# A linear-attention block mixed with a gated MLP: gate and up of both token pairs first, h kept in DRAM, and all down projections as seven block products over three feature groups

## The chip, the cores and the metric

One core of a Trainium2 chip. The time is that of the device in microseconds (us), of the slowest core; the median of 3 runs is 1539.86 us (1535.67 to 1541.33). All data is float32; operands of TensorE are split into a high and a low part of type float32r, and a product of two such operands is the sum of high x high, high x low and low x high.

## The reference

x has 2048 tokens of 576 features. The output mixes a linear attention of 32 heads and a gated MLP with 4608 hidden features by one sigmoid gate per token:

```python
g = sigmoid((x * gate_w).sum(-1, keepdims=True))
# a: linear attention
q, k, v = split_heads(x @ wqkv)
pq, pk = phi(q), phi(k)            # phi(t) = where(t > 0, t + 1, exp(t)) + 1e-6
kv, z = sum_s pk v, sum_s pk
a = merge_heads((pq @ kv) / (pq @ z + 1e-6)) @ wo
# b: gated MLP
h = gelu(x @ w_gate) * (x @ w_up)
b = h @ w_down
return g * a + (1 - g) * b
```

## The kernel before

The instructions stand on each engine in the order in which the program writes them; nothing is reordered. Five engines work at once (TensorE, VectorE, ScalarE, GpSimd, and SP, which issues most transfers), each strictly in its own order, and wait for one another by semaphores.

**Keys, values, queries (to about 180 us).** Projections, Gram matrices and the head states are made; the token blocks are b = 0 to 3, of 512 tokens each.

**Mixing (to about 291 us, L638 to L759 and L1041 to L1054).** For each block: `query(b, g)` projects five head groups and applies phi (ScalarE relu and exp, VectorE), `halves_of` splits the result in high and low (hl), `den` multiplies it by the key sums, `reciprocals` inverts that, writes it to DRAM (rden_d) and loads it spread over the rows (rb), `scaled` multiplies and splits (p), and `mixed(b, t)` makes 128 tokens of the attention's output, which ScalarE scales by the gate and stores to ga_d. The calls are interleaved by hand. Between them `token_sums(kt, part)` makes sums of token blocks 0 and 1 for the MLP: a chunk of 1 MB (xc, one buffer) is loaded, VectorE forms four sums in place, ScalarE copies them to the operand xo (high parts) and GpSimd subtracts (low parts). The first chunk is issued on SP, the next two on GpSimd's queue right behind the subtraction that frees the buffer (L646).

**The MLP (from L1041).** Tokens are taken in two pairs of blocks, p = 0 (tokens 0 to 1023) and p = 1; hidden features in 18 pairs of 128, n = 0 to 17. Gate and up of a pair of blocks by a pair of features are a 2 x 2 block product, done by Winograd's form of Strassen's method: seven products (`product`, 7 matmuls of 512 columns each) in the order SEQUENCE = 1, 6, 2, 7, 5, 4, 3, of sums of token blocks (xo, seven slots) and sums of weight blocks (W[0] = wg for gate, W[1] = wu for up). I call the 49 matmuls of one (p, n, gate or up) a chain. VectorE adds the products up (u2, u3, p1) and multiplies by gelu of the gate; ScalarE makes p1 and gelu.

- First pass, p = 0, n = 0 to 17: the weight sums are made from wgu (SP loads, GpSimd sums and low parts, ScalarE high parts) and stored to wp_d, 2,240 KB each. The down projection of n - 1 is interleaved (`down`): 8 tiles of 128 tokens by 12 matmuls of 288 columns, added by VectorE into acc.
- Beside it `sums_ahead` makes the sums of the second token pair in six pieces, in rounds 2 to 13 (load on SP, sums and low parts on GpSimd, copy on ScalarE, stores on GpSimd's queue), and writes them to xop_d.
- Second pass, p = 1: xo is renewed from xop_d, the weight sums are loaded from wp_d, and for 16 of the 18 rounds the down projection is done by seven products too (`unit`, 84 matmuls of 288 columns per round), each added by VectorE into its own array (sums), which `combine` puts together at the end; rounds 34 and 35 use `down`.

The two splits of weights, `w_fetch`, `w_sums` and `w_split`, use two raw buffers (wgraw, wuraw). PSUM holds four single banks (`bank`) and two pairs of banks (`pair`).

## Time and profile before

| what | value |
|---|---|
| median of 3 runs | 1539.86 us (1535.67 to 1541.33) |
| span of the profiled execution | 1537.6 us |
| mean granted TensorE clock | 0.998 |
| VectorE, ScalarE, GpSimd busy | 1026.0, 542.2, 864.8 us |
| moved by DMA | 279.63 MB, mean 182 GB/s |
| last mixing product to last matmul | 291.65 to 1532.5 us |
| one round of the first pass, of the second | 35.33 us, 33.80 us |

How to read the rows that the prediction shows. The page's first line has busy time, share of the span and number of instructions of each engine; PE is TensorE's matmul, PEld its weight load, DVE VectorE, ACT ScalarE, POOL GpSimd, SP SyncE; SPq and ACTq are the queues on which transfers are issued. Matmuls are pipelined: "busy" spans from a matmul's start to its modelled end, so the mean of one (393 ns for 512 columns) is no price, and two starts must be compared. Rows of the chain of waits have start, length and what ran; rows of the timeline start, length, engine, line, operation, output<-input and in brackets the idle time ahead with what ended it; rows of the stretches the window, its length, busy us and number of instructions of TensorE, weight load, VectorE, ScalarE and GpSimd, then granted clock, DMA share and GB/s; rows of groups the number, busy us and mean ns of one; rows of transfers the number, KB each and median us from issue to landing.

### The profile page before, as it was taken

The page shows a single profiled execution, that of the slowest core. Times are in us where ns is not written, and L with a number is a line of the kernel's source. Part 1 is how long each engine was busy: PE and PEld are TensorE (multiplying, and loading weights), DVE is VectorE, ACT ScalarE, POOL GpSimd, SP SyncE. Part 2 cuts the span into 40 slices and gives each one's busy share as a digit, 9 for nine tenths or more (in the row PEclk, how much of TensorE's full clock was granted, in tenths as well). Part 3 has the DMA queues.
Part 4 walks back from the last instruction along what each step waited for, and adds up shares of the span by engine and source line. Part 5 has one row for each costly group of instructions (what it writes and reads, how often), then busy time and mean ns, then how long its engine had stood idle before and what let it go on. Part 6 is the DMA issues. An engine that isn't in the chain of part 4 may idle for free.

```text
span 1537.6 us, 21533 instructions
## 1 busy us (share of the span) xinstructions
PE 1527.1 (99%) x8594; PEld 1356.8 (88%) x8594; DVE 1026.0 (67%) x1345; ACT 542.2 (35%) x784; POOL 864.8 (56%) x696
## 2 busy tenths in 40 slices
PE   8999999999999999999999999999999999999999
PEld 8998889888888888888888888888888888888888
DVE  7886776465555555565655556777777776777786
ACT  6554555333333333333333332223223222232321
POOL 3653112276777768686756656555666655566631
PEclk9999999999999999999999999999999999999999
DMA  7563225765556565565544584443344334334442
GB/s 239 150 171 139 90 105 194 247 237 191 219 204 240 212 225 204 190 233 187 231 176 186 197 336 182 152 179 136 139 176 167 135 143 185 139 136 165 180 167 93
DMA packets 57884, 279.63 MB, mean 182 GB/s; under 512 B 4912, under 2 KB 22984, under 8 KB 47160
## 3 DMA queue, kind: packets, MB, share of 16 engines
q1 hardware_dynamic: 53032, 261.21, 45.9%
q10 hardware_dynamic: 3024, 9.72, 1.7%
q0 software_dynamic: 1728, 7.34, 1.2%
q8 instruction: 67, 1.10, 0.3%
q14 instruction: 33, 0.27, 0.1%
HBM read 176.77 MB, written 101.47 MB: 181 GB/s over the span
## 4 chain that ended last, share of the span: by engine, by line
PE 91%; DMA 2%; DVE 2%; issue 1%; POOL 1%; ACT 1%; ACTq 0%; SPq 0%; POOLq 0%; DVEq 0%
PE bank L807 52%; PE pair L971 16%; PE pair L1003 12%; PE bank L384 3%; PE pair L239 2%; PE kpair L239 2%; PE pair L194 1%; PE kpair L194 1%; DMA rb<-rden_d 1%; PE pair L629 1%; POOL wv L375 0%; DMA xc<-xs 0%; DMA rden_d<-rb 0%; DVE r L610 0%; PE bank L971 0%
## 5 line engine op out<-in xcount | busy, mean ns | idle before, releaser
L807 PE MATMUL bank<-xo,wu 128*128 128x512 f32 x1764 | 434.8, 393 | 0.0
L807 PE MATMUL bank<-xo,wg 128*128 128x512 f32 x1764 | 433.6, 394 | 0.0
L807 PEld LDWEIGHTS bank<-xo,wg 128*128 128x128 f32 x1764 | 325.2, 188 | 64.0 <-DMA wg<-wp_d 0.2
L807 PEld LDWEIGHTS bank<-xo,wu 128*128 128x128 f32 x1764 | 322.6, 188 | 59.9 <-DVE p L907 0.6
L971 PEld LDWEIGHTS pair<-wd,h 128*128 128x128 f32 x1716 | 243.8, 189 | 13.0 <-DVE h L850 0.4
L971 PE MATMUL pair<-wd,h 128*128 128x288 f32 x1716 | 250.5, 295 | 0.2 <-DVE h L850 0.2
L847 ACT ACTIVATE h<-e 128x512 fp32r<-128x512 f32 x128 | 80.9, 632 | 381.4 <-DVE e L844 354.8
L988 DVE SCALAR_TENSOR_TENSOR acc<-pair,gate,acc 128x576 f32<-128x576 f32 x143 | 116.7, 816 | 128.0 <-PE pair L971 128.0
L1008 DVE TENSOR_TENSOR sums<-pair,sums 128x576 f32<-128x576 f32 x210 | 157.3, 755 | 31.0 <-PE pair L1003 23.8
L850 DVE TENSOR_TENSOR h<-e,h 128x512 fp32r<-128x512 f32 x128 | 124.1, 970 | 44.4 <-ACT h L847 44.3
L877 ACT ACTIVATE e<-e 128x512 f32<-128x512 f32 x108 | 68.1, 630 | 226.3 <-DVE e L933 90.6
L797 POOL TENSOR_TENSOR wdb<-draw,wdb 128x432 fp32r<-128x432 f32 x32 | 36.2, 1153 | 183.7 <-ACT wdb L795 183.7
L1003 PEld LDWEIGHTS pair<-wdb,h 128*128 128x128 f32 x768 | 111.1, 189 | 7.0
L1003 PE MATMUL pair<-wdb,h 128*128 128x288 f32 x768 | 115.4, 296 | 0.0
L722 POOL TENSOR_TENSOR wu<-wuraw,wu 128x768 fp32r<-128x768 f32 x18 | 35.8, 1990 | 117.1 <-ACT wu L721 117.1
L1003 PEld LDWEIGHTS pair<-wdb,hx 128*128 128x128 f32 x576 | 84.0, 189 | 5.5
L1003 PE MATMUL pair<-wdb,hx 128*128 128x288 f32 x576 | 87.2, 296 | 0.0
L882 ACT ACTIVATE p<-bank 128x512 f32<-128x512 f32 x72 | 43.0, 598 | 119.9 <-PE bank L807 118.1
L887 DVE TENSOR_TENSOR u<-bank,p 128x512 f32<-128x512 f32 x72 | 49.4, 687 | 39.4 <-PE bank L807 36.9
L629 PEld LDWEIGHTS pair<-kw,p 126*128 126x128 f32 (+1 forms) x480 | 66.6, 193 | 4.5 <-ACT p L65 2.4
L629 PE MATMUL pair<-kw,p 126*128 126x288 f32 (+1 forms) x480 | 68.4, 301 | 1.9 <-ACT p L65 1.8
L844 DVE TENSOR_TENSOR e<-u,e 128x512 f32<-128x512 f32 x72 | 68.7, 954 | 2.5
(207 smaller groups left out, 2260.3 us busy)
## 6 DMA issues: line engine op xcount, KB each, us to landing
wp_d<-wg SPq DMA_DIRECT2D x17, 2240.0 KB, 6.7
wp_d<-wu SPq DMA_DIRECT2D x17, 2240.0 KB, 8.0
wg<-wp_d SPq DMA_DIRECT2D x17, 2240.0 KB, 8.8
wu<-wp_d SPq DMA_DIRECT2D x17, 2240.0 KB, 8.7
draw<-wdn SPq DMA_DIRECT2D x36, 576.0 KB, 9.3
wgraw<-wgu SPq DMA_DIRECT2D x18, 768.0 KB, 4.2
wuraw<-wgu SPq DMA_DIRECT2D x18, 768.0 KB, 4.3
xo<-xop_d SPq DMA_DIRECT2D x7, 1280.0 KB, 7.1
```

Of the source, the lines that this page charges most:

```text
L239: nc.tensor.matmul(y[:, n, :KH], a, p[:, n * KH:(n + 1) * KH], start=(k == 0), stop=(k == len(ops) - 1))
L629: nc.tensor.matmul(y[:, i, :288], p[:R, a, g], KW[g][:R, wl, i * 288:(i + 1) * 288], start=(n == 0), stop=(n == 14))
L807: nc.tensor.matmul(ps, w_, x_, start=start and i == 0, stop=i == 6, skip_group_check=not start)
L844: nc.vector.tensor_tensor(es[i], v, es[i], OP.mult)
L847: nc.scalar.activation(hs[i][:, 0], es[i], AF.Copy)
L850: nc.vector.tensor_tensor(hs[i][:, 1], es[i], f32(hs[i][:, 0]), OP.subtract)
L877: nc.scalar.activation(es[i], es[i], AF.Gelu_apprx_tanh)
L887: nc.vector.tensor_tensor(u2, b, p1, OP.add)
L971: nc.tensor.matmul(y[i], hs[i0 + f][:, hl, c], wd_of[n][(1 - i, 2 + i)[f]][:, wl], start=(k == 0), stop=(k == 5))
L988: nc.vector.scalar_tensor_tensor(o, v, gate[:, 1, st:st + 1], o, op0=OP.mult, op1=OP.add)
L1003: nc.tensor.matmul(y[:, j, :288], h[:, hl, c], wd[:, b, wl], start=(i == 0), stop=(i == 2))
L1008: nc.vector.tensor_tensor(o, y[:, :, :288], o, OP.add)
```

## The change

Gate and up of both token pairs are now done first, and all down projections after them.

- **Order of chains.** CHAINS lists 72: (0, n = 0), (0, 1), (1, 1), then for n = 2 to 17 gate of both pairs, then up of both, and last (1, 0), whose weights are loaded again from wp_d. Each weight tile is made once and serves both pairs, so only the first (n = 0) is kept in DRAM. The raw weights and their sums have one buffer (in `stage`).
- **h.** The seven blocks of h that the down products need (h itself and its sums) are formed by VectorE in the chain (L885 to L897 of the changed kernel) and stored to h_d by SP, 256 KB each, 252 stores.
- **Second operand.** xo2, the operand of the second token pair, is loaded during the first four chains. So its sums must be ready when the mixing stage ends: `sums_ahead` is called from there, through `next_ahead`, in 13 places, with all its transfers on SP.
- **Chunks.** The second and third chunk of `token_sums` are issued on ScalarE's queue at the start of the call that uses them.
- **Down.** 84 units: six groups s of three feature pairs, two token pairs, seven products; a unit has 36 matmuls of 288 columns (two times two tiles of 128 tokens, three feature pairs, three parts). Sums of products are kept in PSUM: product 1 is copied by ScalarE into a second pair of banks, and the following products are added there by TensorE; six of the seven products are followed by an addition into acc by VectorE. The h block of a unit is loaded by SP six units ahead and split by ScalarE and VectorE three units ahead; the weights of a group are split by ScalarE and GpSimd during the group before.
- PSUM has 8 single banks during gate and up and 4 pairs during down. The sign of T4 is turned, so that product 4 can be added.

```diff
@@ mixing
+    def next_ahead():
+        k, part = divmod(ahead_at[0], 2)
+        ahead_at[0] += 1
+        if part == 0 and k:
+            sums_ahead(k - 1, 2)
+        if k < 6:
+            sums_ahead(k, part)
     def token_sums(kt, part):
         if part == 0:
+            if kt:
+                chunk[0] = Chunk(xcp, 0, kt, nc.scalar)
             chunk[0].sums()
         else:
             chunk[0].summed(nc.gpsimd)
-            if kt < 2:
-                chunk[0] = Chunk(xcp, 0, kt + 1, nc.gpsimd)
...
     query(0, 0)
+    next_ahead()
     query(0, 1)
+    next_ahead()
     den(3, 0)
     halves_of(3, 2)
...
@@ gate and up
+    CHAINS = ([(0, 0, GATE), (0, 0, UP), (0, 1, GATE), (0, 1, UP), (1, 1, GATE), (1, 1, UP)] +
+              [(p, n, m) for n in range(2, NF2) for m in range(2) for p in range(NP)] +
+              [(1, 0, GATE), (1, 0, UP)])
...
+        def s4():
+            e = bank()
+            product(p, 4, m, e, True)
+            block(2, u3, e, u3)
+            if m == UP:
+                nc.vector.tensor_tensor(sx[:, 0], es[2], es[3], OP.add)
+                nc.vector.tensor_tensor(sx[:, 1], sx[:, 0], es[0], OP.subtract)
+                nc.vector.tensor_tensor(es[2], es[0], es[2], OP.subtract)
+                keep_block(S1, sx[:, 0])
+                keep_block(S2, sx[:, 1])
+                keep_block(S3, es[2])
...
+            if i == 0 and c in at:
+                n, m = at[c]
+                w_split(m)
+                if (n, m) != (NF2 - 1, 1):
+                    w_fetch(n + m, 1 - m)
+            for k in XO2_AT.get((c, i), ()):
+                a = PRODUCTS[SEQUENCE[k]][0]
+                nc.sync.dma_start(f32(X[1][:, a]), xop_d[:, a])
+            if i == 0 and c == LAST - 3:
+                w_load(0)
+            if i == 0 and c == LAST - 1:
+                w_load(1)
+            if (c, i) == (LAST - 3, 1):
+                d_fetch(0)
+            if (c, i) == (LAST - 2, 0):
+                h_load(0)
+                d_make(0, 0)
...
@@ down
+    for j in range(4, 6):
+        h_load(j)
+    for p in range(NP):
+        for t in range(8):
+            i, j = divmod(t, 4)
+            nc.sync.dma_start(acc[p][:, 2 * i:2 * i + 2, j], ga_d[p * 8 + t].rearrange("p (n c) -> p n c", n=2))
...
+        for j in range(2):
+            t = 2 * q + j
+            ops = [(hl, wl, g) for hl, wl in ((0, 0), (0, 1), (1, 0)) for g in range(3)]
+            for n, (hl, wl, g) in enumerate(ops):
+                nc.tensor.matmul(y[:, j, :288], h[:, hl, g, t * 128:(t + 1) * 128], w[:, wl, g * 288:(g + 1) * 288],
+                                 start=k in (1, 5) and n == 0, stop=n == len(ops) - 1, skip_group_check=True)
+            if c is not None:
+                st = p * 8 + c // 2 * 4 + t
+                o = acc[p][:, c, t]
+                nc.vector.scalar_tensor_tensor(o, y[:, j, :288], gate[:, 1, st:st + 1], o, op0=OP.mult, op1=OP.add)
...
+    for u, (s, p, k) in enumerate(UNITS):
+        unit(u, 0)
+        h_make(u + 3)
+        h_load(u + 6)
+        unit(u, 1)
+        if u < 3:
+            d_make(0, u + 4)
```

Three places show how the order of instructions moves.

ScalarE in the mixing stage, from `query(0, 0)` to the second `scaled` (r is a query, hl its halves, p the scaled query, xuh the high part of a piece of the second pair's sums). Before:

```order
L386 ACTIVATE r<-bank 126x512
L387 ACTIVATE r<-r 126x512
L514 ACTIVATE hl<-r 126x512 x2
L386 ACTIVATE r<-bank 126x512
L387 ACTIVATE r<-r 126x512
L514 ACTIVATE hl<-r 72x512
L65 ACTIVATE p<-r 126x640
L386 ACTIVATE r<-bank 126x512
L387 ACTIVATE r<-r 126x512
L65 ACTIVATE p<-r 126x640
```

The same place now:

```order
L392 ACTIVATE r<-bank 126x512
L393 ACTIVATE r<-r 126x512
L657 ACTIVATE xuh<-xu 128x1024
L520 ACTIVATE hl<-r 126x512 x2
L392 ACTIVATE r<-bank 126x512
L393 ACTIVATE r<-r 126x512
L520 ACTIVATE hl<-r 72x512
L65 ACTIVATE p<-r 126x640
L392 ACTIVATE r<-bank 126x512
L393 ACTIVATE r<-r 126x512
L657 ACTIVATE xuh<-xu 128x1024
L65 ACTIVATE p<-r 126x640
```

Two copies of pieces now stand ahead of halves and of a scaled query; four more follow further on.

SP at the same time (rden_d and rb are the reciprocals' trip through DRAM, xu the raw piece, xul and xuh its low and high part). Before, the reciprocals alone:

```order
L594 DMA rden_d_70<-rb 35x256
L594 DMA rden_d_71<-rb 35x256
L598 DMA rb<-rden_d_70 126x1x1280
L598 DMA rb<-rden_d_71 126x1x1280
L594 DMA rden_d_72<-rb 35x256
```

Now:

```order
L604 DMA rb<-rden_d_67 126x1x1280
L604 DMA rb<-rden_d_68 126x1x1280
L651 DMA xu<-xs 128x4x256
L667 DMA xop_d<-xul 128x4x256
L668 DMA xop_d<-xuh 128x4x256
L651 DMA xu<-xs 128x4x256
L667 DMA xop_d<-xul 128x4x256
L668 DMA xop_d<-xuh 128x4x256
L651 DMA xu<-xs 128x4x256
L600 DMA rden_d_69<-rb 35x256
```

Behind the first two reciprocal loads three loads of pieces now stand on SP, each but the first behind the stores of the piece before it.

SP at the end of gate and up (h_d is h in DRAM; e and f hold h of the first and second token pair, sx its sums; xo here is the place of an h block that is loaded back). Before, in the second pass, a weight load stands behind two other loads:

```order
L769 DMA draw_8276<-wdn 128x1152
L729 DMA wg<-wp_d_0_97 128x4480
L729 DMA wu<-wp_d_1_98 128x4480
L769 DMA draw_8276<-wdn 128x1152
L729 DMA wg<-wp_d_0_99 128x4480
```

Now:

```order
L969 DMA xo<-h_d_1_91 128x1536
L839 DMA h_d_5_101<-f_3223 128x512
L839 DMA h_d_5_101<-sx 128x512 x2
L839 DMA h_d_5_101<-f_3222 128x512
L839 DMA h_d_5_101<-f_3221 128x512
L839 DMA h_d_5_101<-sx 128x512
L826 DMA wu<-wp_d_89 128x4480
L969 DMA xo<-h_d_1_91 128x1536 x2
L839 DMA h_d_0_96<-f_3220 128x512
```

The load of the up weights for the last chain stands behind all stores of the last chain of feature pair 17.

More of the change, by code (lines that the diff above doesn't have):

```diff
@@ L736, in tile_gated_mix @@
     scaled(0, 0)
-    nc.scalar.dma_start(f32(W[0]), wp_d[0][0])
+    nc.scalar.dma_start(f32(W[0]), wp_d[0])
     mixed(3, 3)
@@ L833, in renew, with w_fetch @@
-    def renew(i):
-        a = PRODUCTS[SEQUENCE[i]][0]
-        nc.sync.dma_start(f32(xo[:, a]), xop_d[:, a])
-    def gu_steps(m, seam=False, blocks=False):
-        ps = {}
+    def w_fetch(n, m):
+        nc.sync.dma_start(wraw, wgu[n, m])
+        b12, b11, b21, b22 = (wraw[:, i] for i in range(4))
+        t1, t2, t3, t4 = (tsum[:, i] for i in range(4))
+        for o, a, b in ((t1, b12, b11), (t2, b22, t1), (t3, b22, b12), (t4, b21, t2)):
+            nc.gpsimd.tensor_tensor(o, a, b, OP.subtract)
@@ L1047, in tile_gated_mix @@
     scaled(1, 0)
-    nc.scalar.dma_start(f32(W[1]), wp_d[0][1])
+    nc.scalar.dma_start(f32(W[1]), wp_d[1])
     first_steps[3]()
```

514 lines of the change are left out of this document (189 added, 325 removed).

## The prediction

> **What bounds the kernel now.** I read the page first (busy shares, chain by engine), then the chain of waits in order of time, then the timeline of each engine where the chain leaves TensorE.
>
> ```profile
> PE 1527.1 (99%) x8594; PEld 1356.8 (88%) x8594; DVE 1026.0 (67%) x1345; ACT 542.2 (35%) x784; POOL 864.8 (56%) x696
> PE 91%; DMA 2%; DVE 2%; issue 1%; POOL 1%; ACT 1%; ACTq 0%; SPq 0%; POOLq 0%; DVEq 0%
> 291.81 22.68 PE bank L807 x98
> 338.52 11.29 PE bank L807 x49
> 373.85 11.29 PE bank L807 x49
> 1007.40 9.66 PE bank L807 x42
> 1041.20 9.66 PE bank L807 x42
> 1526.07 6.40 PE pair L971 x48
> ```
>
> The chain gives true prices. 49 matmuls of 512 columns take 11.29 us, 0.2304 each. One round of the first pass lasts 373.85 - 338.52 = 35.33 us: 98 such (22.58) and 96 of 288 columns, so these cost 12.75/96 = 0.1328. A round of the second pass lasts 33.80 and has 84 of them: 0.1336. By these prices all gate, up and down work left after 291.65 (1,240.9 us) just fills the time to the last matmul at 1532.5. From there to the end TensorE is the bound, with no slack to find. Before that, in the mixing stage, other engines carry the chain:
>
> ```profile
> 187.81 1.09 PE L524 MATMUL den<-hl,zmk 126*128 126x512 f32 x4
> 253.12 8.14 PE L629 MATMUL pair<-kw,p 126*128 126x288 f32 x60
> 281.72 10.09 PE L629 MATMUL pair<-kw,p 126*128 126x288 f32 x60 [1.77 <-ACT p L65]
> 218.68 5.82 DMA xc<-xs
> 268.85 11.20 DMA rb<-rden_d
> 280.00:285.00 5.00, 3.21 (x15) 2.98 (x16) 3.21 (x4) 2.10 (x3) 0.00 (x0) 0.79 0.87 358
> 285.00:290.00 5.00, 5.00 (x35) 5.00 (x34) 0.00 (x0) 0.74 (x1) 0.00 (x0) 0.87 0.26 105
> ```
>
> The load of xc and the trip of the reciprocals through DRAM (rb) stand on the chain of waits, so what delays VectorE or these loads here delays the stage's end one for one. The last rows show a second cost of a gap: after 1.77 us without work the granted clock was 0.79 and 0.87, and 60 matmuls took 10.09 us instead of 8.14.
>
> **What the change removes.** The order of instructions has 3,264 matmuls of 288 columns before and 3,024 after (12 passes of 7 products, 36 matmuls each); gate and up keep 3,528. Before: 1,920 x 0.1328 + 1,344 x 0.1336 = 434.5 us; after, between 401.6 and 404.0. I take **-31.7** (-30.5 to -32.9). A chain (gate or up, 49 matmuls) stays at 11.29 us, a unit (36 matmuls) costs 4.8.
>
> **Mixing: the six pieces.** The sums of the second token pair, made beside gate and up before, now stand in the mixing stage. Each piece (512 KB) needs: a load on SP, four sums on GpSimd, one copy on ScalarE, four differences on GpSimd, one or two stores on SP; and xu has one buffer, so SP issues the next load only behind those stores. The copy stands in ScalarE's order in front of work that TensorE waits for.
>
> ```profile
> 150.00:200.00 50.00, 50.00 (x243) 39.95 (x242) 33.94 (x59) 28.14 (x51) 4.28 (x3) 1.00 0.28 110
> GB/s 239 150 171 139 90 105 194 247 237 191 219 204 240 212 225 204 190 233 187 231 176 186 197 336 182 152 179 136 139 176 167 135 143 185 139 136 165 180 167 93
> 183.51 1.89 SPq L598 DMA_DIRECT2D rb<-rden_d  x2
> 184.48 0.63 ACT L387 ACTIVATE r<-r 126x512 f32<-126x512 f32 x1
> 185.02 1.14 ACT L514 ACTIVATE hl<-r 126x512 fp32r<-126x512 f32 x2
> 214.97 0.63 ACT L514 ACTIVATE hl<-r 126x512 fp32r<-126x512 f32 x1 [0.40 <-PE bank L384]
> 426.29 0.59 SPq L817 DMA_DIRECT2D xu<-xs  x1
> 435.09 0.74 POOL L553 TENSOR_TENSOR xu<-xu 128x256 f32<-128x256 f32 x1 [5.06 <-DMA xu<-xs]
> 437.54 0.74 POOL L556 TENSOR_TENSOR xu<-xu 128x256 f32<-128x256 f32 x1
> L822 ACT ACTIVATE xuh<-xu x6: 1040/1042/1047, 385.9 to 739.1; 128x1024 fp32r<-128x1024 f32 x6
> xop_d<-xuh POOLq DMA_DIRECT2D x6, 512.0 KB, 3.9
> ```
>
> The first load follows the rb loads on SP: issued at 185.4. Landing 3.9 us (the store of the same size): 189.3. Four sums, 437.54 + 0.74 - 435.09 = 3.2: 192.5. ScalarE came to this place at 185.1, so it stands for 7.4 us, and the hl copies that den (TensorE at 187.81) needs come behind it. Then a cycle: copy 1.04, differences 3.2, two stores and the next load, sums 3.2. Two stores and a load: 3.9 for the first, and 1.56 for each other 512 KB at the best slice of the GB/s row (336) = 7.0; cycle 14.4. Bounds: all three overlapped, 3.9 (cycle 11.3); or the landing seen behind a 2,240 KB store, 435.09 - 426.29 = 8.8 (cycle 16.2). The fourth copy starts at 192.5 + 3 x 14.4 = 235.7 and ends at 236.7; the hl copy behind it started at 214.97 before: **+21.7** (+12.5 to +27). TensorE shows no gap there (50.00 of 50 us), so it cannot catch up.
>
> The Trainium skill, page "DMA: Bandwidth & Descriptors", section "Anatomy of one DMA — SWDGE (gpsimd) path", puts a transfer at about 2.0 us plus bytes over 436 GB/s. For 1.57 MB that is 5.6 us instead of 7.0, an estimate, three cycles 4.2 us shorter, and the sum would end at 1559. No run here shows three such transfers in a row, so the rows decide.
>
> **Mixing: the chunk loads.** The second and third chunk (xc, 1 MB) were issued by GpSimd as soon as the buffer came free; now ScalarE issues them just ahead of VectorE's sums, which then wait for the whole landing, with all of VectorE's work queued behind.
>
> ```profile
> 222.06 0.74 ACT L65 ACTIVATE p<-r 126x640 fp32r<-126x640 f32 x1 [1.08 <-DVE r L610]
> 224.59 0.69 DVE L553 TENSOR_TENSOR xc<-xc 128x512 f32<-128x512 f32 x1 [0.93 <-DMA xc<-xs]
> 247.47 0.33 ACTq L737 DMA_DIRECT2D wg<-wp_d  x1
> 250.48 0.61 ACT L514 ACTIVATE hl<-r 72x512 fp32r<-72x512 f32 x1
> 251.95 0.68 DVE L553 TENSOR_TENSOR xc<-xc 128x512 f32<-128x512 f32 x1
> wg<-wp_d SPq DMA_DIRECT2D x17, 2240.0 KB, 8.8
> ```
>
> Second chunk: issue behind p at 222.80, landing 5.8 later, 228.6 against 224.59: +4.0, and up to 4.7 more because a piece's 1.57 MB moves at the same time; I take +5.5 (4 to 8.7). Third: issue at 251.1 against sums at 251.95, landing at 256.7, or 259.4 if it runs behind the 2,240 KB load issued at 247.47 on the same queue: +6.3 (4.8 to 7.5). The fifth and sixth piece, where GpSimd also splits a chunk in between: +1 (0 to 3). Mixing in sum **+34.5** (21 to 46).
>
> **Gate and up.** The second pair's operand (7 loads of 1,280 KB, 9.2 MB) must land in some 39 us beside two weight fetches, its last three loads behind a fetch that waits for GpSimd; at 336 GB/s that just fits: **+2** (0 to one landing, 7.1). In the steady part nothing ends later than TensorE: an up chain has 13 VectorE operations of about 0.69, 9.4 us of 11.29, and after two such come two gate chains with five; weight preparation on GpSimd gets 22.6 us for each of the tiles of which it makes two in 35.33 now.
>
> ```profile
> xo<-xop_d SPq DMA_DIRECT2D x7, 1280.0 KB, 7.1
> L902 DVE TENSOR_TENSOR u<-bank,u 128x512 f32<-128x512 f32 x72 | 49.3, 685 | 15.1 <-PE bank L807 14.3
> L844 DVE TENSOR_TENSOR e<-p,e 128x512 f32<-128x512 f32 x36 | 42.2, 1172 | 1.2
> L66 DVE TENSOR_TENSOR wd<-draw,wd 128x1152 fp32r<-128x1152 f32 x18 | 24.5, 1359 | 11.0 <-ACT wd L65 11.0
> L988 DVE SCALAR_TENSOR_TENSOR acc<-pair,gate,acc 128x576 f32<-128x576 f32 x143 | 116.7, 816 | 128.0 <-PE pair L971 128.0
> 291.05 8.05 SPq L949 DMA_DIRECT2D acc<-ga_d  x8
> ```
>
> **The last chains.** The up weights of the first feature pair come back (2,240 KB, 8.8 us) for the last chain, but SP issues that load behind the h stores of the chain two before it, and the last of those waits for VectorE. From the start of the two last ordinary up chains: 3.2 us to the first VectorE operation, 26 operations (18.7 with gaps), one difference of an h block (1,359 ns for 1,152 columns, so 1.8 for 1,536), 3.5 waiting for that block and some 4 waiting for products: 31. Landing 40; the last chain was due at 3 x 11.29 = 33.9: **+6** (0 if VectorE keeps up, 12 if its operations cost 1,172 ns).
>
> **Start of the down phase.** SP issues, behind the last chain's stores, two h blocks (768 KB), sixteen acc tiles, and only then the block for the seventh unit. Eight acc tiles took 8.05 us: some 4 + 5 + 16 + 4 = 29 us to landing, 33 with copy and difference, while VectorE stands in front of evictions that the second half of the sixth unit (due at 26) needs: +6, and +2 for the first evictions, which wait for acc: **+8** (2 to 14). In the steady part VectorE has 1.8 + 24/7 x 0.51 = 3.5 of 4.8 us per unit (an eviction of 288 columns lies between 0.41 and 0.82 by L988).
>
> **Clock.** The two stalls in which TensorE is the bound afterwards each lose what the 1.77 us gap lost, 10.09 - 8.14 = 2: **+4** (0 to 8). By the Trainium skill, page "TensorE: Matmul & The Clock Gate", section "Part 1: The HAM clock gate", an idle window of about 3.4 us halves the clock until a busy one has passed, an estimate of 1.7 us each; the trace agrees in kind, though its gap was shorter.
>
> **Sum.** -31.7 + 34.5 + 2 + 6 + 8 + 4 = +22.8. The profiled span is 1537.6; the median of the runs lies 2.3 above it, and I carry that over: 1537.6 + 22.8 + 2.3 = **1563**. All low ends together give 1530, all high ends 1597.
>
> **Rivals.** (1) The waits for the pieces are hidden: TensorE has enough queued work, or a cycle is under 9.8 us (29.5 us between ScalarE's first and fourth place, over three), and only the chunk loads are paid. -31.7 + 11.8 + 2 + 3 + 2 = -13: 1527, faster. For it: GpSimd was idle here. Against it: ScalarE runs in order, and den needs the very copies behind the wait. (2) Short cycles and low ends: -31.7 + 21 + 6 + 5 = 0: 1540. (3) The down phase runs at VectorE's pace: sums now stay in PSUM, so a product may not start before the eviction two units back. If evictions cost 0.82, 1.8 + 4 x 0.82 = 5.1 against 4.8 in 72 units: +21 more, 1584 or beyond. Against it: the mean has room. (4) 3,024 matmuls don't get cheaper in sum, because each costs more: the two kinds of down differ by 0.6% today, so worth 2.4 us at most.
>
> **Chances.** Forecast 0.70 (its own range 1549 to 1580), rival 1 0.10, rival 2 0.12, rival 3 0.07, others 0.01. The range to 1545 and 1583 leaves most of rivals 1 and 2 outside. What can be told from no change is 0.5%, 7.7 us: slower 0.77, same 0.13, faster 0.10.
>
> **What would show it.** In the profile of the changed kernel: ScalarE idle in front of the xuh copy, put down to GpSimd, 7 us and then 5 to 9 for the next three; VectorE idle in front of the sums of the second and third chunk, put down to the DMA; the last product of the mixing stage near 326 instead of 291.65; chains of 11.29 and units of 4.8 us; TensorE waiting for wu at the last chain, and in the first six units. I am wrong if mixing ends before 310, or if a unit takes over 5 us.

## The result: 1780.66 us, 15.7% slower

The changed kernel takes 1780.66 us (median of 4 runs, 1779.36 to 1781.64) against 1538.88 us for the kernel before on the same chip: ratio 1.1573, 95% interval 1.1551 to 1.1594. The prediction was 1563 (1545 to 1583): the sign is right, the size is off by some 218 us.

From the page of the changed kernel: span, busy times, TensorE's busy tenths in 40 slices, the chain by engine, and the group of the evictions.

```profile
span 1779.4 us, 21486 instructions
PE 1560.1 (88%) x8354; PEld 1345.8 (76%) x8354; DVE 975.2 (55%) x1314; ACT 542.9 (31%) x685; POOL 697.9 (39%) x536
PE   9999676999999999999999999877777777777776
PE 19%; DVE 12%; issue 3%; ACT 1%; DMA 0%; SPq 0%; DVEq 0%; ACTq 0%
L1047 DVE SCALAR_TENSOR_TENSOR acc<-pair,gate,acc 128x288 f32<-128x288 f32 x288 | 148.5, 516 | 278.8 <-PE pair L1042 273.4
```

TensorE was busy 99% of the span before and is now busy 88%. Its row has two dents: slices 5 to 7 (178 to 311 us, the mixing stage) and everything from slice 27 on (1157 us, the down phase). The second is the larger by far, and no engine is full there. VectorE, which alternates with TensorE in the chain that ended last, is busy 55%. An alternation of two engines of which neither is full points to a wait for each other, and not to an engine that is too slow.

The waits name it (engine, line, what it waited for: us in total, times, longest):

```profile
PE pair L1042 <- DVE acc L1047: 161.5, 144, 6.4
POOL xu L559 <- DMA xu<-xs: 52.0, 5, 21.1
ACT xuh L657 <- POOL xu L562: 47.5, 6, 13.3
DVE xc L559 <- DMA xc<-xs: 11.5, 2, 7.3
```

144 is 12 passes x 6 products that are followed by an eviction x 2 halves: one wait of TensorE in every half of such a unit. TensorE's timeline through one unit late in the down phase, and VectorE's beside it (start, us, and in brackets the idle time before and what ended it):

```profile
1488.63 1.35 PE L1042 MATMUL pair<-wd,wu 128*128 128x288 f32 x9
1490.59 2.66 PE L1042 MATMUL pair<-wd,wu 128*128 128x288 f32 x18 [0.61 <-DVE acc L1047]
1494.76 1.46 PE L1042 MATMUL pair<-wd,wu 128*128 128x288 f32 x9 [1.51 <-DVE acc L1047]
1496.06 1.36 PE L1042 MATMUL pair<-xo 128*128 128x288 f32 x9
...
1490.02 0.52 DVE L1047 SCALAR_TENSOR_TENSOR acc<-pair,gate,acc 128x288 f32<-128x288 f32 x1 [0.67 <-PE pair L1042]
1492.10 0.52 DVE L1047 SCALAR_TENSOR_TENSOR acc<-pair,gate,acc 128x288 f32<-128x288 f32 x1 [1.56 <-PE pair L1042]
1492.53 1.75 DVE L975 TENSOR_TENSOR xo<-hraw,xo 128x1536 fp32r<-128x1536 f32 x1
1494.20 0.51 DVE L1047 SCALAR_TENSOR_TENSOR acc<-pair,gate,acc 128x288 f32<-128x288 f32 x1
```

A unit of 36 matmuls takes 1496.06 - 1488.63 = 7.43 us instead of 4.8. Nine matmuls write the first token tile (j = 0), then VectorE evicts it (1490.02 to 1490.54), and only then do the nine of the second token tile (j = 1) begin (1490.59): both tiles lie in one PSUM tile of two banks, and the matmul that writes one half of it waits for the eviction that reads the other. In the second half the eviction itself stands behind the split of a later h block (L975, 1.75 us), so TensorE stands for 1.51 us in front of the next nine and not for 0.61. The kernel before had no such place: there one instruction evicts both halves of a pair, behind the matmuls of both (L988 in the prediction's rows, 576 columns).

The rest of TensorE's timeline, in the mixing stage and at the start of the down phase:

```profile
198.01 2.77 PE L530 MATMUL den<-hl,zmk 126*128 126x512 f32 x4 [12.09 <-ACT hl L520]
334.69 9.51 PE L635 MATMUL pair<-kw,p 126*128 126x288 f32 x60 [3.19 <-ACT p L65]
1139.45 3.35 PE L808 MATMUL bank<-xo,wu 128*128 128x512 f32 x7 [5.31 <-DVE p L846]
1166.38 6.12 PE L1042 MATMUL pair<-xo 128*128 128x288 f32 x45
1178.86 4.69 PE L1042 MATMUL pair<-xo 128*128 128x288 f32 x18 [6.36 <-DVE acc L1047]
```

The last product of the mixing stage ends at 344.2 (before: 291.65 by the last row of that stage), 52 us later and not 34.5. Gate and up then run to 1166.38, and the down phase from there to 1776, 610 us for matmuls worth 401.6 to 404.0.

### The profile page after: what moved, and what is told of

The parts are those of the page before. It is cut to its first block, busy times and chain, and to the rows that moved or that the text cites. A ratio compares the mean times of both kernels' runs of the same rounds, so it can differ in the third digit from the quotient of the medians.

```text
span 1779.4 us, 21486 instructions
## 1 busy us (share of the span) xinstructions
PE 1560.1 (88%) x8354; PEld 1345.8 (76%) x8354; DVE 975.2 (55%) x1314; ACT 542.9 (31%) x685; POOL 697.9 (39%) x536
## 5 line engine op out<-in xcount | busy, mean ns | idle before, releaser
L1047 DVE SCALAR_TENSOR_TENSOR acc<-pair,gate,acc 128x288 f32<-128x288 f32 x288 | 148.5, 516 | 278.8 <-PE pair L1042 273.4
L1042 PE MATMUL pair<-xo 128*128 128x288 f32 x1044 | 156.6, 303 | 59.5 <-DVE acc L1047 59.5
L1042 PEld LDWEIGHTS pair<-xo 128*128 128x128 f32 x1044 | 142.9, 191 | 71.4 <-DVE acc L1047 71.3
L816 POOL TENSOR_TENSOR stage<-stage 128x384 f32<-128x384 f32 x136 | 163.5, 1222 | 50.7 <-DMA stage<-wgu 48.0
L1042 PE MATMUL pair<-wd,xo 128*128 128x288 f32 x792 | 121.8, 309 | 38.4 <-DVE acc L1047 38.4
L822 POOL TENSOR_TENSOR wg<-stage,wg 128x768 fp32r<-128x768 f32 (+1 forms) x34 | 72.3, 2126 | 192.3 <-ACT wg L821 191.0
L1042 PEld LDWEIGHTS pair<-wd,xo 128*128 128x128 f32 x792 | 112.0, 197 | 47.1 <-DVE acc L1047 47.1
L822 POOL TENSOR_TENSOR wu<-stage,wu 128x768 fp32r<-128x768 f32 (+1 forms) x34 | 79.3, 2333 | 136.8 <-ACT wu L821 135.4
L1042 PE MATMUL pair<-wd,wu 128*128 128x288 f32 x396 | 59.6, 302 | 20.2 <-DVE acc L1047 20.2
L1042 PE MATMUL pair<-xo,wg 128*128 128x288 f32 x360 | 55.5, 304 | 21.4 <-DVE acc L1047 21.4
```

Of the source, the lines that this page charges most:

```text
L816: nc.gpsimd.tensor_tensor(o, a, b, OP.subtract)
L822: nc.gpsimd.tensor_tensor(w[:, i, 3:5], src[:, :, 0:2], f32(w[:, i, 0:2]), OP.subtract)
L1042: nc.tensor.matmul(y[:, j, :288], h[:, hl, g, t * 128:(t + 1) * 128], w[:, wl, g * 288:(g + 1) * 288], start=k in (1, 5) and n == 0, stop= ...
L1047: nc.vector.scalar_tensor_tensor(o, y[:, j, :288], gate[:, 1, st:st + 1], o, op0=OP.mult, op1=OP.add)
```

## The experiments

Times are medians, each against the kernel before on the same chip (1536.5 to 1539.1 in these sets). The sets ran on different chips, so a difference between runs of two sets is known to 2 or 3 us only.

**1. Two tiles of one bank.** The accumulators of the two token tiles become two PSUM tiles. No instruction is moved; only ScalarE's copy of product 1 becomes two copies, one for each tile.

```diff
-            sums_of[name, q] = pair()
+            sums_of[name, q] = [bank() for _ in range(2)]
...
-                nc.tensor.matmul(y[:, j, :288], h[:, hl, g, t * 128:(t + 1) * 128], w[:, wl, g * 288:(g + 1) * 288],
+                nc.tensor.matmul(y[j][:, :288], h[:, hl, g, t * 128:(t + 1) * 128], w[:, wl, g * 288:(g + 1) * 288],
```

> In the down products each token tile gets an accumulator tile of its own (one PSUM bank each, two instead of one tile of two banks), nothing else is moved. Theory: the second token tile of a half unit waits for the eviction of the first because both lie in one PSUM tile; with two tiles the 144 waits of TensorE for the eviction go, a unit falls from 7.4 to about 4.8 us, some 2.5 x 72 = 182 us less: about 1600 us (1585 to 1620). Rival, VectorE's pace (the third rival of the prediction): the evictions themselves are the bound, so units stay over 7 us and the time within 20 us of 1781. Rival, half of each: the split of the next h block still holds up the products, units of about 6 us, 1680.

1575.1 us, 205.6 below the change (ratio to before 1.0243, 1.0226 to 1.0260).

**2. The tile of two banks, evictions later.** Both evictions of a half are issued behind its 18 matmuls.

```diff
         for j in range(2):
...
-            if c is not None:
-                st = p * 8 + c // 2 * 4 + t
+        if c is not None:
+            for j in range(2):
+                t = 2 * q + j
+                st = p * 8 + c // 2 * 4 + t
```

> The accumulator tile of two banks stays, but the two evictions of a half unit are issued behind the matmuls of both token tiles, so no matmul of the half stands behind an eviction of the same half. Theory (wait inside the tile): as with two tiles, units of about 4.8 us and about 1600 us (1585 to 1620); the same number of evictions of the same size, so VectorE has no less to do. Rival, VectorE's pace: within 20 us of 1781, since VectorE gets its work later, not earlier. If this is fast and the two tiles are not, or the other way round, the theory falls.

1579.2 us (1.0271, 1.0236 to 1.0306; the four runs spread from 1573.3 to 1586.0). So the number of tiles is not what counts: the same tile, the same 288 evictions, and the wait inside the half is gone.

**3. The split between the evictions.** As the change, but the h block's split is issued between the first half's two evictions.

```diff
-        unit(u, 0)
-        h_make(u + 3)
+        unit(u, 0, lambda: h_make(u + 3))
```

> The tile of two banks and the evictions stay as in the change; only the split of the h block three units ahead (ScalarE copy, VectorE difference of 1.75 us) moves from behind the second eviction of the first half to between its two evictions. Theory: the 1.0 us by which that difference delays the first eviction of the second half goes (1.77 falls to 0.76), the wait for the eviction itself stays: 72 x 1.0 = 72 us less, about 1708 us (1695 to 1725), units of about 6.3 us. Rival, VectorE's pace: the same work in another order, within 10 us of 1781.

1732.5 us (1.1270, 1.1252 to 1.1287): 48 less, two thirds of the 72 expected, and the wait for the eviction stays (144 waits, 117.0 us in sum). The windows show the four kernels in the middle of the down phase (busy time in 100 us of TensorE, its weight loads, VectorE, ScalarE, GpSimd; then granted clock, DMA share, GB/s): the change, two tiles, the later evictions, and the moved split.

```profile
1480.00:1580.00 100.00, 73.06 (x496) 67.31 (x495) 48.25 (x62) 27.41 (x24) 26.82 (x22) 0.98 0.39 129
```

```profile
1300.00:1400.00 100.00, 100.00 (x757) 100.00 (x756) 71.55 (x94) 42.00 (x43) 33.16 (x25) 1.00 0.59 202
```

```profile
1300.00:1400.00 100.00, 100.00 (x757) 100.00 (x756) 69.36 (x95) 43.74 (x38) 37.97 (x29) 1.00 0.56 184
```

```profile
1300.00:1400.00 100.00, 78.66 (x542) 72.30 (x541) 57.00 (x69) 30.71 (x27) 36.02 (x29) 1.00 0.41 136
```

496 matmuls in 100 us are 7.26 us for a unit, 757 are 4.76, 542 are 6.64. With two tiles VectorE is busier (72%) than in the change (48%), because it has the same work in less time; with the later evictions it is busy 69%. VectorE's pace, the third rival, falls with that.

**4 and 5. The mixing stage without the pieces.** In the first, loads, sums, copies and differences of the pieces are left out (a blank tile is stored); in the second the chunks are also loaded early from GpSimd's queue, as before the change. Both keep the slow down phase.

```diff
-        if part == 0:
-            raw = ahead[k] = xup.tile([128, 4, HB], F32, name="xu")
...
-        else:
-            hi, lo = ahead.pop(k)
+        if part == 2:
+            lo = hi = blank
```

```diff
         else:
             chunk[0].summed(nc.gpsimd)
+            if kt < 2:
+                chunk[0] = Chunk(xcp, 0, kt + 1, nc.gpsimd)
```

> The six pieces are left out of the mixing stage but for their stores: no load, sums, copy or differences, and a blank tile is stored, so the second pair's sums are zeros. Theory: the pieces cost some 40 of the 52 us by which the mixing stage ends later than before, the chunk loads the rest (11.8 by the prediction): the last product of the mixing stage at about 304 instead of 344.2, total about 1740 us (1732 to 1748). Rival: the chunk loads and the changed order cost most of it, and the stage ends at 320 or later (over 1755 us); or the pieces cost all of it: 292, 1728.

> The change with its accumulator tile of two banks, the pieces left out but for stores of a blank tile (the second pair's sums are zeros), and the chunks loaded early from GpSimd's queue as before the change. Theory: of the 52 us the pieces were 44 and the late chunk loads the other 8; without both, the mixing stage ends where it did before, at 292 (to 295), and the time is 1728 us (1724 to 1732). Rival: something else of the change (SP, the order) costs the rest: within 3 us of 1736.

1735.96 and 1732.26 us. The pieces cost 44.7 us. Without them the largest gap of the stage is 9.94 us, where p waits behind VectorE and the third chunk (first row); with the chunks early that gap is gone, one of 4.82 comes later (second row), and the last product ends at 293.2, within 2 us of before. By the medians that is 3.7 us, by the two spans (1734.2 and 1729.2) 5.0; the runs of the second spread over 9 us, so the chunks' cost is known to a few us only.

```profile
265.51 6.60 PE L635 MATMUL pair<-kw,p 126*128 126x288 f32 x30 [9.94 <-ACT p L65]
```

```profile
283.15 10.05 PE L635 MATMUL pair<-kw,p 126*128 126x288 f32 x60 [4.82 <-ACT p L65]
```

**6 to 9. Who carries the pieces' cost.** All with two accumulator tiles (1575.1). The copies go to GpSimd; or xu gets a second buffer and the loads run a cycle ahead; or the chunks alone come early; or everything of the pieces goes to GpSimd, transfers too, with the second buffer and the chunks early (of this last one the edit is not shown).

```diff
-            nc.scalar.activation(hi, raw, AF.Copy)
+            nc.gpsimd.tensor_copy(hi, raw)
```

```diff
+    def piece_load(k):
+        if k < 6:
+            raw = ahead[k] = xup.tile([128, 4, HB], F32, name="xu", bufs=2)
+            nc.sync.dma_start(raw, xs[1, k // 2, :, :, k % 2 * HB:(k % 2 + 1) * HB])
...
             sums_ahead(k - 1, 2)
+            piece_load(k + 1)
...
     chunk = [Chunk(xcp, 0, 0)]
+    piece_load(0)
+    piece_load(1)
```

> On top of the two accumulator tiles: the high parts of the six pieces are copied by GpSimd instead of ScalarE, in the same places of the order, so ScalarE no longer stands behind a piece's load and sums. Theory: the pieces cost their 44 us because ScalarE, in order, waits for them with the copies that TensorE needs queued behind; without that wait the mixing stage ends near where it ends without pieces (300), and the time falls from 1575 to about 1535 (1528 to 1545). Rival, the queue: SP holds the loads of the reciprocals behind the piece's stores, and GpSimd's splits of the chunks come later; then at most half of it, 1555 or more. Rival, contention of the added DMA and GpSimd work: no gain, 1570 or more.

> On top of the two accumulator tiles: xu gets a second buffer, the first two pieces are loaded ahead of the reciprocals' trips and each later load a cycle earlier; the copies stay on ScalarE in their places. Theory: of the wait of ScalarE per piece (13.3, 6.3, 8.6, 3.2, 8.5, 7.6 us) the landing (some 5 to 10 us each) goes and the sums (3.2) stay in part; the mixing stage ends some 25 to 35 us earlier, about 1545 us (1538 to 1555). Rival: the cycle is set by the stores and GpSimd's work and not by the load's landing, then under 10 us gained, 1565 or more.

> On top of the two accumulator tiles: the second and third chunk are again loaded from GpSimd's queue as soon as the buffer is free, as before the change. Theory: the waits of VectorE for the two chunks (4.2 and 7.3 us) go, but the pieces behind still set part of the pace, so between those 11.5 us and nothing: about 1568 us (1562 to 1575). Rival: the issue on GpSimd comes no earlier, since GpSimd splits the chunk before only late, behind pieces: 1573 or more, no difference.

> On top of the two accumulator tiles, the pieces are kept wholly to GpSimd: two buffers with loads a cycle ahead, the high parts copied by GpSimd, loads and stores issued from GpSimd's own queue, and the chunks loaded from there as soon as their buffer is free. Theory as the runs so far leave it: a piece costs time through every engine whose queue it stands in, ScalarE (the copy), SP (the reciprocals' stores held behind the piece's stores, 219.3 instead of some 203 with the copies on GpSimd) and ScalarE again (the chunk's load issued behind a split that GpSimd does late); with all three free, the mixing stage ends near 295 to 305, against 318.8 with the loads ahead alone: about 1530 us (1524 to 1540), below the kernel before. Rival, GpSimd becomes the carrier (some 12 us a piece, 70 us, and the chunks' splits behind): the stage ends at 315 or later, 1547 or more.

1567.3, 1549.7, 1569.9 and 1566.6 us. Taking the copies off ScalarE, which the theory held for the carrier, gained 8 us of 45. The rows of that run say why: the reciprocals' store on SP (L600) is issued at 219.31, behind a piece's stores, and VectorE waits for the load that follows it; and ScalarE itself stands 13.0 us in front of r, because the chunk's load it is to issue waits for GpSimd's split (L577), which comes behind a piece.

```profile
219.31 1.44 SPq L600 DMA_DIRECT2D rden_d<-rb  x2
...
229.90 1.18 DVE L616 SCALAR_TENSOR_TENSOR r<-r,rb 126x640 f32<-126x640 f32 x1 [6.74 <-DMA rb<-rden_d]
```

```profile
ACT r L392 <- POOL xo L577: 13.0, 1, 13.0
```

With everything on GpSimd, that engine is the carrier: TensorE idles 24.9 us because VectorE stands 25.47 us in front of a chunk. The load of that chunk is issued only behind the split of the one before, which GpSimd reaches at 242.78, since its transfers, issued one behind the other, wait 2.7 to 5.6 us each (first the waits of its queue, then the issue of the chunk).

```profile
POOL xu L671 <- issue: 16.9, 5, 5.6
POOL xop_d L666 <- issue: 14.2, 4, 4.6
```

```profile
248.02 0.57 POOL L570 DMA_DIRECT2D xc<-xs  x1 [0.32 <-POOL xo L577]
...
257.36 0.80 PE L530 MATMUL den<-hl,zmk 72*128 72x512 f32 x1 [24.90 <-DVE hl L521]
```

**10 to 12. The stalls at the last chains and the start of down.** First the first two h blocks made three steps and one step later, and the second pair's acc loads later; then, on top of the GpSimd version (1566.6), the three blocks made much later, with the same acc loads; last (with loads ahead and the sixth piece first, 1536.2) the first block one step later.

```diff
-            if (c, i) in ((LAST - 2, 3), (LAST - 1, 2), (LAST, 1)):
+            if (c, i) in ((LAST - 2, 6), (LAST - 1, 3), (LAST, 1)):
...
+        if u == 1:
+            acc_loads(1)
```

> On top of the two accumulator tiles: the first two h blocks are made some steps later in the last chains, and of the sixteen acc loads the eight of the second token pair are issued only in the second unit, the first eight between the two h loads. Theory: the stall of 4.4 us near 1131 is VectorE standing in front of the difference of the first h block while that block's load is under way (not the reload of the up weights, as the prediction had it), and the 3.6 us near 1190 is the h load behind the acc loads; both go, 1567 us (1564 to 1571). Rival: the waits only move, 1573 or more.

> The same with the start of the down phase changed too: the first three h blocks are made in the last but one and the last chain, each after its load can have landed, the second pair's acc loads in the second unit. Theory: the stalls near 1131 (4.4 us) and 1190 (3.6 us) are VectorE in front of an h block whose load is under way; made later, they cost nothing: 6 to 8 us below the run without it, about 1523 us (1515 to 1535). Rival: they only move, as in the run that moved them by three and one steps (no gain), within 2 us of it.

> The same with the first h block made one step (1.6 us) later in the last but two chain. Theory: of the 3.2 us that TensorE still loses near 1097, where VectorE stands in front of that block's difference with the load under way until 1096.2, two thirds go: 2 us less than without it. Rival: the next block then comes later and the gap moves: within 1 us, or slower.

1574.7, 1564.6 and 1538.0 us: against 1575.1, 1566.6 and 1536.2, nothing that a median tells. The stall moves with the split. In the change VectorE stands 4.54 us in front of the first block's difference; three steps later TensorE stalls 8.25 us one chain on; made later still, it waits for wu and for ScalarE.

```profile
1136.13 2.67 DVE L975 TENSOR_TENSOR xo<-xo 128x1536 fp32r<-128x1536 f32 x1 [4.54 <-ACT xo L974]
```

```profile
1154.55 3.35 PE L808 MATMUL bank<-xo,wg 128*128 128x512 f32 x7 [8.25 <-DVE f L843]
```

```profile
1137.93 13.26 PE L814 MATMUL bank<-xo,wu 128*128 128x512 f32 x49 [3.26 <-DMA wu<-wp_d]
1162.81 8.69 PE L1050 MATMUL bank<-xo 128*128 128x288 f32 x54 [4.46 <-ACT bank L1061]
```

**13 to 16. Orders that free one queue after another.** On two banks and loads ahead (1549.7): the chunks loaded from SP; then also the first h block's load issued by ScalarE instead of SP, and the acc loads of the second pair in the second unit; then the sixth piece's sums and the fifth's stores ahead of the second chunk's split; then the chunks from GpSimd, which issues only these two transfers in the stage.

```diff
-                chunk[0] = Chunk(xcp, 0, kt, nc.scalar)
+                chunk[0] = Chunk(xcp, 0, kt + 1, nc.sync)
...
-                h_load(0)
+                h_load(0, nc.scalar)
...
+    next_ahead()
     token_sums(1, 1)
     query(1, 3)
-    next_ahead()
...
-                chunk[0] = Chunk(xcp, 0, kt + 1, nc.sync)
+                chunk[0] = Chunk(xcp, 0, kt + 1, nc.gpsimd)
```

> On top of the two accumulator tiles and the pieces' loads a cycle ahead on SP (1549.7): the second and third chunk are loaded from SP's queue as soon as GpSimd has split the chunk before, so neither ScalarE (in order behind its copies) nor GpSimd (3 to 5 us for each transfer it issues) carries them. Theory: VectorE's two waits for the chunks, 11.9 us there, cost TensorE the gaps of 5.1 and 5.8 us and the lower clock behind each; they go: 1540 us (1534 to 1545). Rival: GpSimd's split comes so late behind the pieces that the load starts no earlier, 1547 or more.

> The same, and the load of the first h block is issued by ScalarE instead of SP, where it stands behind the h stores of the chain before, and the acc loads of the second pair come in the second unit. Theory: the stall near 1131 is that load's late issue (SP 1128.7, while the operand it overwrites was free some 8 us before), and that near 1190 the h load behind sixteen acc loads: 5 to 8 us less, 1533 us (1527 to 1540), not slower than the kernel before. Rival: the transfers of this stretch as a whole are the limit, so the stall moves again, within 2 us of the run without it.

> On top of the run that equals the kernel before (1537.6): the sixth piece's sums and the fifth's stores come ahead of the second chunk's split and the third chunk's load. Theory: what is left of the pieces is mainly one wait of ScalarE, 11.3 us in front of the sixth copy, because the fifth's store stands on SP behind the third chunk's load, which waits for GpSimd's split (issued 246.7), and TensorE idles 7.1 us at 249 for the hl copy queued behind; with the store first that gap goes to 1 or 2 us: 1530 us (1525 to 1534), below the kernel before. Rival: the chunk's split and load, now later, take its place: 1535 or more.

> On top of the run with the sixth piece first (1536.2): the chunks are loaded from GpSimd's queue, right behind the split that frees their buffer, so SP no longer holds the reciprocals' store (ready at 246, issued at 251.7) and loads behind it. Theory: the last gap, 6.4 us in front of p at 265 with the lower clock behind it, is this store's wait on SP; GpSimd issues a single transfer in about 0.6 us, only rows of them cost 3 to 5 us each. 4 to 7 us less: 1531 us (1528 to 1534), 0.4% below the kernel before. Rival: the gap moves again (the third chunk's landing, or the reciprocals' trip itself), within 2 us of 1536.

1542.7, 1537.6, 1536.2 and 1530.3 us. The third missed: its order removed ScalarE's wait of 11.3 us, but the reciprocals' store then stood on SP behind the chunk's load, and a gap of 6.4 us came up later in the stage. The last run, which frees SP of the chunk's load, took that gap to 1.66, and is 0.53% faster than the kernel before (ratio 0.9947, 0.9930 to 0.9963), just over what can be told from no change. Its busy times, and the gap:

```profile
PE 1505.8 (98%) x8354; PEld 1327.7 (87%) x8354; DVE 984.2 (64%) x1314; ACT 545.8 (36%) x709; POOL 732.1 (48%) x538
268.48 6.05 PE L635 MATMUL pair<-kw,p 126*128 126x288 f32 x30 [1.66 <-ACT p L65]
```

## Why the prediction was wrong

The sign was right, and for the reason given: without the wait inside the PSUM tile the change takes 1575.1 us. That lies inside the predicted range, but in part by luck: pieces and chunks cost 50.2 us by the spans and not 34.5, gate and up with the last chains 14.9 and not 8, while the start of the down phase took 3.6 and not 8, and the clock's 4 is inside the other terms.

By the spans of the runs the 241.8 us (1779.4 - 1537.6) close: -31.7 (matmuls) + 205.0 (wait inside the PSUM tile, 1779.4 - 1574.4) + 45.2 (pieces, 1779.4 - 1734.2) + 5.0 (chunks) + 14.9 (gate and up, 821.3 from 345.03 to 1166.38 instead of 806.4 for 3,500 matmuls) + 3.6 (an h load at the start of down, left with two banks) = 242.0. The small terms are not independent of each other, so that it closes to 0.2 us is chance. Of the 205.0 the rows of the waits name 161.5; they count from the modelled end of a matmul (nine last 1.35 us from the first start to it), which lies behind the point at which a next one could start.

- **The steady down phase, costed at nothing: the step that failed, 205 us.** The prediction's words were "In the steady part VectorE has 1.8 + 24/7 x 0.51 = 3.5 of 4.8 us per unit". That sum is right: the eviction takes 0.516 us, the split 1.75, and with two banks VectorE is busy 72%. Wrong was to ask only whether VectorE has time. The question was what TensorE's next matmul waits for, and how long ahead of it the thing is done. The answer stood in the diff: one `pair()` tile holds both token tiles, and the eviction of j = 0 stands in the program in front of the matmuls of j = 1. I had taken an eviction to be due a unit or more later, at the next product on that accumulator. The mean room of 1.3 us a unit is no cover for a wait that begins and ends inside half a unit. In its place the runs showed one wait of TensorE in each of the 144 halves, units of 7.26 us, and 4.76 once the second token tile no longer waits for the first.
- **Rival 3** had the right place and half of the symptom ("units over 5 us") but another mechanism, VectorE's pace, and so the price of 21 us. Experiments 1 and 2 exclude it: the same 288 evictions, and units of 4.76 us.
- **The pieces, +21.7 and +1: mechanism right, size wrong by half (45.2).** ScalarE does wait in front of the first copy with den's copies queued behind (12.09 us at TensorE). Two terms are mis-sized. The first load's landing was taken as 3.9 from a store of the same size: issued at 183.36, it let GpSimd begin at 193.22, 9.9 later. The upper bound set for it was 8.8, so the bound was not a bound. With the four differences, which took 3.4 to 5.0 us and not 3.2, this puts the fourth copy at 243.45 instead of 235.7: 7.7 us of the 22 that are missing. Two stores and a load took 6.2 to 7.7 us from the first issue to the sums, near the 7.0 of the sum.

```profile
183.36 0.62 SPq L651 DMA_DIRECT2D xu<-xs  x1
193.22 0.72 POOL L559 TENSOR_TENSOR xu<-xu 128x256 f32<-128x256 f32 x1 [21.09 <-DMA xu<-xs]
196.38 1.06 ACT L657 ACTIVATE xuh<-xu 128x1024 fp32r<-128x1024 f32 x1 [13.32 <-POOL xu L562]
243.45 1.06 ACT L657 ACTIVATE xuh<-xu 128x1024 fp32r<-128x1024 f32 x1 [3.21 <-POOL xu L562]
```

  The larger part lies behind the fourth copy. The waits of ScalarE were 13.3, 6.3, 8.6, 3.2, 8.5 and 7.6 us: the fifth and sixth piece, put at +1, hold it for 16.1. And ScalarE was only one of three queues that carried the cost, which the prediction had not seen. The 5.6 us for two stores and a load, by the Trainium skill, page "DMA: Bandwidth & Descriptors", section "Anatomy of one DMA — SWDGE (gpsimd) path", come from a fit for transfers that GpSimd issues; these, issued by SP, took 6.2 to 7.7.
- **The chunk loads, +11.8.** VectorE's two waits are 4.2 and 7.3 us, 11.5 in sum, as predicted; at the end they are worth some 4 to 5, since they overlap the pieces' waits or, without these, TensorE's queued work. (251.1 + 5.8 is 256.9 and not 256.7, which changes nothing.)
- **Matmuls, -31.7.** Right: with two banks the down phase is 1163.69 to 1571, 407.4 us with a stall of 3.55, against 401.6 to 404.0. (The 1532.5 of the table is the end of the chain of waits; the last matmul of the kernel before ends at 1534.06, so some 1.5 us of its MLP are not accounted for by these prices.)
- **Gate and up, +2, with chains of 11.29: too low.** The operand of the second pair landed in time; TensorE's longest wait in the first chains, once they run, is 0.45 us. But in the steady part two chains start 22.75 us apart, 11.37 each, which over 72 chains is 6 of the 14.9 us. TensorE has no gap there (200.00 of 200 us from 500 to 700) and the granted clock is 1.00, so no run here shows why; the cause stays open.

```profile
498.71 22.91 PE L808 MATMUL bank<-xo,wg 128*128 128x512 f32 x98
521.46 22.91 PE L808 MATMUL bank<-xo,wu 128*128 128x512 f32 x98
```

- **Last chains, +6.** The stall is there (5.3) but for another reason: not wu, whose load is in time in the change, but VectorE in front of the first h block's difference while that block lands. The transfers of this stretch shift it from place to place; issuing the first load some 3 us earlier (by the distance to VectorE's work beside it) together with the acc order gained 5.1 in experiment 14, with 3.2 and 1.8 us of the two stalls left; its two parts were not tried apart.
- **Start of down, +8.** The mechanism is as predicted: with two banks the seventh unit's block is issued on SP behind the sixteen acc loads, VectorE stands 6.84 us in front of its difference, and TensorE loses 3.55 us. The first evictions, put at +2, wait for acc: in the change TensorE loses 6.36 us by it, with two banks nothing, though VectorE still stands 5.73 us there.

```profile
1169.15 13.31 SPq L1022 DMA_DIRECT2D acc<-ga_d  x16
1182.72 0.39 SPq L969 DMA_DIRECT2D xo<-h_d  x1
...
1191.41 1.76 DVE L975 TENSOR_TENSOR xo<-xo 128x1536 fp32r<-128x1536 f32 x1 [6.84 <-ACT xo L974]
...
1193.65 10.04 PE L1042 MATMUL bank<-wd,xo 128*128 128x288 f32 x54 [3.55 <-DVE acc L1047]
```

- **Clock, +4.** For the two stalls that it was meant for, right. Behind the 5.31 us the granted clock was 0.50 and seven matmuls took 3.35 us, against 1.91 for the seven at 1153.18; behind the 6.36 us it was 0.50 too, and eighteen took 4.69 against 2.65 for the next eighteen. What the sum had at nothing is the clock in the mixing stage. The first two rows are that stage before and in the change (the clock is the third number from the end, 0.98 and 0.84): TensorE is busy 121.05 us for 658 matmuls where it was 110.06 for 669, an estimate of 13 us of slower matmuls out of the stage's 52. The third row shows one of the places: thirty matmuls that take 4.14 us at full clock.

```profile
180.00:292.00 112.00, 110.06 (x669) 99.25 (x668) 67.26 (x87) 51.65 (x78) 19.02 (x16) 0.98 0.45 161
```

```profile
180.00:345.00 165.00, 121.05 (x658) 105.95 (x656) 69.69 (x85) 56.54 (x81) 63.21 (x63) 0.84 0.45 156
```

```profile
228.99 7.03 PE L635 MATMUL pair<-kw,p 126*128 126x288 f32 x30 [6.03 <-ACT p L65]
```

The warning sentence "I am wrong ... if a unit takes over 5 us" named the right row. It should have had a price.

The Trainium skill, page "Perfetto Trace Analysis", section "Matmuls", says that independent matmul groups should rotate through different PSUM banks, so that the evacuation of one overlaps the matmuls of the next. The runs agree in effect and add a condition: the two token tiles were in different banks all along, and still 27% of TensorE's time was lost in the window shown, since the wait was kept for the tile of two banks. The Trainium skill, page "PSUM — Partial Sum Buffer", section "PSUM bank collisions raise a hardware error", asks to guard PSUM by bank; one tile for each bank does just that, and gave 100.00 of 100 us.

## What to carry to other kernels

For every instruction of the bound engine ask which instruction releases it and how many instructions of the bound engine lie between the two; an engine that is busy less than half of the time (48% here) can still stop another one twice in each unit if its work is asked for at once. Where one PSUM tile holds two independent results, evict both behind the matmuls of both, or give each its own tile. Work that is spread over in-order queues costs through each queue it stands in, so taking it off one of them may show little (7.8 us with the copies off ScalarE), and the gains came step by step: 25, 32 and, with the start of down, 45 us as loads, chunks and stores no longer waited for one another.

## What the hardware showed that was not expected

- **Short gaps in a dense rhythm left the clock nearly alone.** In the change's down phase TensorE was idle 27% of the time in gaps of 0.6 and 1.5 us, and the granted clock was 0.98. Before the change one gap of 1.77 us in the mixing stage was followed by 0.50 from 283 to 286 us (the 0.79 and 0.87 of the prediction are means over 5 us); in the change one of 1.64 us was followed by 1.00 (216 to 219.7). So no run here gives a length from which the clock falls.
- **Transfers issued by GpSimd one behind the other** waited: of ten, nine stood 2.69 to 5.56 us before their issue (31.1 us in sum); the tenth, behind a chunk's load, did not. A chunk's load alone was issued in 0.57. No run here shows why.
- **VectorE and GpSimd slow each other.** In the change, sums of 512 columns with two operands take 1.22 to 1.10 us while GpSimd works on its differences (228.39 to 232.67), and 0.69 when it has ended. GpSimd's four differences take 4.28 us there, and 2.80 in experiment 6 at a place where VectorE has nothing to do (213.18 to 221.32; last row). The Trainium skill, page "SBUF — State Buffer", section "SBUF: two separate sides", has a pair of ports that VectorE takes for instructions with two operands in SBUF and GpSimd takes for its own, one at a time; these rows agree in kind, since both engines' instructions are stretched.

```profile
228.39 4.28 POOL L660 TENSOR_TENSOR xul<-xu,xuh 128x256 fp32r<-128x256 f32 x4 [1.17 <-ACT xuh L657]
...
229.73 1.22 DVE L559 TENSOR_TENSOR xc<-xc 128x512 f32<-128x512 f32 x1
230.97 1.11 DVE L560 TENSOR_TENSOR xc<-xc 128x512 f32<-128x512 f32 x1
232.12 1.10 DVE L561 TENSOR_TENSOR xc<-xc 128x512 f32<-128x512 f32 x1
233.25 0.69 DVE L562 TENSOR_TENSOR xc<-xc 128x512 f32<-128x512 f32 x1
```

```profile
214.60 2.80 POOL L660 TENSOR_TENSOR xul<-xu,xuh 128x256 fp32r<-128x256 f32 x4
```
